# Softmax normalisation of seven groups and five weight casts moved to GpSimd, with a new order of the whole program

## The chip, the cores and the metric

The kernel runs on one core of a Trainium2 chip. The metric is the device time of one execution in microseconds. The core has five engines that work side by side, each through its own list of instructions in order: TensorE (PE in the profile; its weight loads are PEld), VectorE (DVE), ScalarE (ACT), GpSimd (POOL) and SyncE (SP), which here issues most DMAs. An instruction waits where something that it needs is not there yet, and everything behind it on its engine waits with it.

## The reference

Local attention with block summaries, and behind it a feed-forward network with a squared ReLU:

```python
k_sum = k.reshape(B, H, nb, block, D).max(axis=3)
v_sum = v.reshape(B, H, nb, block, D).mean(axis=3)
scores_l = scale * (q @ k^T), kept where |i - j| < 16
scores_s = scale * (q @ k_sum^T) + log(32)
a = softmax(concatenate([scores_l, scores_s]))
x = a @ concatenate([v, v_sum])      # 4 batches, 8 heads, 768 tokens, 64 wide
h = x @ w_in                         # 3072 tokens, 512 -> 2048
out = (max(h, 0) ** 2) @ w_out       # 2048 -> 512
```

Everything is float32; weights and activations are split into a high part and a low part, the rest, and each product is done as three.

## The kernel before

The tokens are cut into 48 groups of 64 (`g`), all heads of a group together. Per group the kernel does: scores on TensorE (`S`), the masked maximum on VectorE (`X` or `M`), exponentials with their sums on ScalarE (`E`), the reciprocal of the sums on VectorE (`R`), the normalisation of the probabilities (`N`), their transposition on TensorE (`T`) with a copy back by ScalarE (`A`), and the product with the values on TensorE (`V`). The result goes as high and low part (`XH` on ScalarE, `XL` on VectorE) into the buffers `xh` and `xl`. `KC` copies the 24 key maxima beside the next group's keys, on GpSimd; the scores of the next group wait for it. `LS` copies the 24 value sums beside a group's values; GpSimd does six of these copies.

Eight groups make a unit of 512 tokens. Units 0 and 1 go through the network plainly, in 16 steps (`FI` into the hidden layer, ReLU `RL`, square `SQ`, high part `GH`, low part `GL`, and `FO` out of it). The first two steps of unit 0 are halved, `a` for groups 0 to 3 and `b` for groups 4 to 7, so that work can begin before all eight groups are done. The last four units are done in two pairs by a folded scheme with seven products of half size instead of eight; its products (`SP`, `FP`) start when unit 1 is through, in the same PSUM banks, which the copies `PC` have to empty first.

A weight block is loaded as raw 64-bit words (`WL`) and turned into a high and a low part: `WM` rebiases the exponent on ScalarE, `WR` shifts the low word and `WJ` joins both on VectorE, `WH` makes the high part on ScalarE (line 1148), `WW` the low part on VectorE.

No loop sets the order. Every piece of work is a task with a due time, a cost and its predecessors; a planner (`Plan.order`) runs through time and lets each engine take the ready task with the smallest key. What it takes is written out, and each engine executes its list in this order. The due times come from constants (`T0`, `VISITS`, `SUMS`, `COMBS` and others), and a table `NUDGE` shifts single tasks.

The normalisation has three forms, chosen for each group by a letter of `NORMAL_BY`. On VectorE (`D`, line 911) it is one multiplication with the reciprocals spread over 118 columns each; on ScalarE (`A`) and on GpSimd (`P`) it is four instructions. No group has the letter `P` before the change. Its form is:

```python
def normal_by_pool():
    for p in range(NPAIR):
        x = pr.tile[:, p, :KEYS]
        nc.gpsimd.tensor_scalar(
            out=x, in0=x, scalar1=nm.tile[:, 2 * NPAIR + p : 2 * NPAIR + p + 1], scalar2=None, op0=ALU.mult
        )
```

Of the kernel before, what the change touches and what calls it, by code (L numbers as in the profile page):

```python
# [42 lines left out]
FIRST_LS = -147  # L43
# [7 lines left out]
NORMAL_BY = 'DDDDDDDDDDDDAADDDDDAADDADAAAADADDADAADADAAAAADAA'  # L51
NUDGE = {
# [15 lines left out]
SUMS_AT = (49.58, 98.461, 159.985)  # L68
HALVED = 2
TURN_LATE = 0.4  # L70
COMBS = (113.899, 126.88, 138.513, 154.582, 177.64, 218.83, 204.98, 217.58)
Q_LEAD = 2.06
XS_LEAD = 6
R_LEAD = 59
TR_LEAD = -6.51
VISITS = (50.338, 57.836, 69.578, 80.836, 104.683, 120.84, 136.81, 147.692, 155.7, 174.797, 185.163, 207.631, 229.485, 242.25, 269.184, 274.88, 306.59, 333.33, 368.58, 382.85, 404.251, 380.898, 406.82)
X_LEAD = 32.91
SPLIT_AT = -65.86
KEPT = (107.051, 3.085)
GH_LEAD = 10  # L80
# [117 lines left out]
class Plan:  # L198
# [14 lines left out]
        KC=(0.2, 0.2), LS=(0.5, 0.5), LD=(0.4, 0.4), N=(0.3, 1.4),  # L213
# [142 lines left out]
def attention_then_relu2_ffn(  # L356
# [95 lines left out]
    T0, SLOW, STEP = 23.88, 6.38, 6.62  # L452
    MIXED_STEP = (1.651, 1.487)
    X_BY = (19.133, 7.867)
    SUMS = (113.265, 126.664, 155.006, 159.6, 204.148, 201.393, 199.633, 202.628, 150.871, 186.465, 171.605, 168.63, 184.229, 220.694, 192.63, 206.893)
    PRODUCT_STEP = (1.392, 1.383)
    A0, A1, B0, B1 = 2.8, 4.14, 31.36, -0.93
    HALF_AT = (26.697, 30.498)
# [350 lines left out]
    def softmax(g, by_pe=False):  # L809
# [8 lines left out]
        one = g < ONE_EXP  # L818
        if g < EARLY + 2:

            t_c = add(
                f"C{g}", "POOL", 0.15, lambda: nc.gpsimd.memset(pr.tile[:, :, KEYS:], 0.0), due - 16,
                [] if early else t_S[g][:1], take=[] if early else [pr], use=[pr] * early, behind=t_QL[g],
            )
        for i, t_s in enumerate(t_S[g]):
# [38 lines left out]

# [236 lines left out]
    def convert(f, ns):  # L1101
# [16 lines left out]
        def temp():  # L1118
            return t.tile[:, : k * DM]
# [45 lines left out]
        t6 = add(f"WH{name}", "ACT", 0.08 + 0.43 * k, high, due - 6, [t4], take=[w], use=[t])  # L1165
# [11 lines left out]
    def ffn(u, f, o, done, half=None):  # L1177
# [34 lines left out]
        t4 = add(f"GH{name}", "ACT", act, lambda: nc.scalar.copy(out=cut(gh), in_=cut(r)), due + 5, [t3], take=[gh], use=[r])  # L1212
# [782 lines left out]
```

## Time and profile before

| | before |
|---|---|
| median of 3 runs | 574.42 us (572.8 to 574.7) |
| profiled execution | 573.33 us |
| its span, first to last instruction | 571.5 us |
| TensorE busy in the span | 558.2 us (98%) |
| VectorE busy | 466.0 us (82%) |
| ScalarE busy | 373.5 us (65%) |
| GpSimd busy | 46.7 us (8%) |
| mean granted TensorE clock | 0.999 of its full speed |

The busy share of an engine is an average over stages with different limits. What a change in a stage is worth is read from that stage: which engine is full there, and which wait ends last.

### The profile page before, as it was taken

How to read it: one execution, taken by the hardware profiler on the slowest of the kernel's cores; microseconds unless marked ns; L12 is line 12 of the kernel's file. 1: busy time of each engine (PE TensorE's matmuls, PEld its weight loads, DVE VectorE, ACT ScalarE, POOL GpSimd, SP SyncE). 2: the span in 40 equal slices, each digit the busy share in tenths (PEclk: the TensorE clock that was granted, in tenths of full speed). 3: DMA queues.
4: the chain of work that ended last, by engine and by line, in shares of the span. 5: the costliest groups of instructions: out<-in, count | busy, mean ns of one | idle time of the engine just before them, and what ended most of it. 6: DMA issues, size and time to landing. Idle time of an engine off the chain costs nothing.

```text
span 571.5 us, 11786 instructions
## 1 busy us (share of the span) xinstructions
PE 558.2 (98%) x3920; PEld 457.6 (80%) x3920; DVE 466.0 (82%) x1182; ACT 373.5 (65%) x968; POOL 46.7 (8%) x95
## 2 busy tenths in 40 slices
PE   7989999999999999999999999999999999999996
PEld 6668888878888888878788888888888888888885
DVE  4999999677899999989998997887583556868863
ACT  2899999577786978697766757465365542454442
POOL 4410031311001130000020000000000000000000
PEclk9999999999999999999999999999999999999999
DMA  8999999989999999999999887968975766767772
GB/s 295 377 397 358 324 288 295 291 234 379 385 293 326 299 370 358 343 350 335 285 278 298 257 266 212 280 194 262 273 212 162 187 197 189 195 193 233 189 233 96
DMA packets 86789, 157.01 MB, mean 275 GB/s; under 512 B 9064, under 2 KB 30506, under 8 KB 86730
## 3 DMA queue, kind: packets, MB, share of 16 engines
q1 hardware_dynamic: 85001, 151.70, 81.3%
q0 software_dynamic: 1728, 4.57, 5.1%
q8 instruction: 31, 0.51, 0.4%
q14 instruction: 29, 0.23, 0.1%
HBM read 112.00 MB, written 49.79 MB: 283 GB/s over the span
## 4 chain that ended last, share of the span: by engine, by line
PE 91%; DVE 4%; DMA 3%; issue 0%; ACT 0%; SPq 0%; DVEq 0%
PE o L1523 23%; PE o L1225 15%; PE o L1740 14%; PE h L1201 14%; PE sz L1740 7%; PE att L1523 4%; PE x L1011 4%; PE att L759 3%; PE sa L1740 3%; PE att L1740 2%; DMA q<-qW 1%; DMA kb<-kT 1%; DMA fv_lent<-vS 1%; DVE qvpa_lent L911 1%; PE o L759 1%; PE t L940 1%
## 5 line engine op out<-in xcount | busy, mean ns | idle before, releaser
L1505 ACT CAST gh<-g 128x512 fp32r<-128x512 f32 x112 | 69.4, 622 | 64.7 <-DVE gl L1510 31.7
L1523 PE MATMUL o<-gh,w 128*128 128x512 f32 x384 | 103.0, 390 | 0.0
L1510 DVE TENSOR_TENSOR gl<-g,gh 128x512 fp32r<-128x512 f32 x112 | 76.4, 687 | 27.2 <-ACT gh L1505 26.6
L1523 PEld LDWEIGHTS o<-gh,w 128*128 128x128 f32 x384 | 71.8, 188 | 15.0
L1201 PE MATMUL h<-xh,w 128*128 128x512 f32 x240 | 74.7, 392 | 0.0
L1777 ACT ACTIVATE g<-g 128x512 f32<-128x512 f32 x60 | 37.7, 631 | 46.9 <-DVE g L1773 46.8
L890 ACT ACTIVATE p<-p,small 128x118 f32<-128x118 f32 x160 | 61.7, 393 | 2.0 <-DVE small L833 2.0
L1225 PE MATMUL o<-w,gh 128*128 128x512 f32 x240 | 61.8, 393 | 0.0
L1523 PE MATMUL o<-gl,w 128*128 128x512 f32 x192 | 59.1, 389 | 0.0
L1201 PEld LDWEIGHTS h<-xh,w 128*128 128x128 f32 x240 | 44.5, 188 | 9.3
L1225 PEld LDWEIGHTS o<-w,gh 128*128 128x128 f32 x240 | 44.4, 188 | 9.3
L1201 PE MATMUL h<-xl,w 128*128 128x512 f32 x120 | 46.8, 390 | 0.0
L1523 PEld LDWEIGHTS o<-gl,w 128*128 128x128 f32 x192 | 36.0, 188 | 7.5
L1740 PE MATMUL o<-w,w 128*128 128x512 f32 x160 | 41.1, 393 | 0.3 <-DVE g L1765 0.3
L1740 PEld LDWEIGHTS o<-w,w 128*128 128x128 f32 x160 | 29.7, 188 | 6.8 <-DVE g L1765 0.7
L1740 PE MATMUL sz<-xh,w 128*128 128x512 f32 x128 | 34.2, 389 | 0.0
L1225 PE MATMUL o<-w,gl 128*128 128x512 f32 x120 | 33.6, 389 | 0.0
L833 DVE CUSTOM_DVE_ANT_0 p<-att,mask 128x118 f32<-128x118 f32 x152 | 32.7, 274 | 0.0
L1500 DVE TENSOR_TENSOR g<-g 128x512 f32<-128x512 f32 x48 | 32.4, 683 | 0.1
L1773 DVE CUSTOM_DVE_ANT_0 g<-sz,g 128x512 f32<-128x512 f32 x32 | 21.9, 684 | 12.3 <-ACT g L1760 6.9
L890 ACT ACTIVATION_READ_ACCUMULATOR p<-p,small 128x1 f32 x160 | 31.5, 197 | 0.0
L1740 PE MATMUL o<-xh,w 128*128 128x512 f32 x112 | 30.2, 391 | 0.8 <-DVE os L1262 0.8
(193 smaller groups left out, 1096.6 us busy)
## 6 DMA issues: line engine op xcount, KB each, us to landing
raw<-wW SPq DMA_DIRECT2D x32, 512.0 KB
w<-scr_t SPq DMA_DIRECT2D x64, 256.0 KB
w<-scr_s SPq DMA_DIRECT2D x64, 256.0 KB
w<-scr_a SPq DMA_DIRECT2D x48, 256.0 KB
w<-scr_i SPq DMA_DIRECT2D x44, 256.0 KB
turn<-a SPq DMA_DIRECT2D x17, 512.0 KB
scr_t<-ci SPq DMA_DIRECT2D x16, 512.0 KB
v<-vS SPq DMA_DIRECT2D x34, 192.0 KB
```

Source lines behind the costliest of these rows:

```text
L759: nc.tensor.matmul(score_at(g, part, j)[c * TQ : (c + 1) * TQ, :], lhsT=q_bufs[g].tile[rows, p, :] if term else unscale[rows, :], rhs=(mas ...
L833: nc.vector.tensor_tensor_reduce(out=pr.tile[:, j, :KEYS], in0=score_at(g, 0, j), in1=mask_of(g)[0], scale=-SCALE, scalar=-NEG, op0=ALU.ad ...
L890: nc.scalar.activation(x, score_tile(g, p % parts)[:, p] if by_pe else x, AF.Exp, bias=nm.tile[:, p : p + 1], scale=SCALE if by_pe else -1 ...
L1011: nc.tensor.matmul(x_of(i)[h % 2 * D : (h % 2 + 1) * D, h // 2, :], lhsT=v_bufs[g].tile[:KEYS, h * D : (h + 1) * D], rhs=av[:KEYS, 2 * c : ...
L1201: nc.tensor.matmul(cut(h), lhsT=lhs.tile[:, k // 2, k % 2 * P : (k % 2 + 1) * P], rhs=rhs[:, k, c0 : c0 + n], start=(i == 0), stop=(i == 3 ...
L1225: nc.tensor.matmul(o_of(o, t).rearrange("p (h c) -> p h c", h=2), lhsT=terms[i][0].tile[:, (t - t0) * P : (t - t0 + 1) * P], rhs=terms[i][ ...
L1500: lambda x=x, ins=ins, op=op: nc.vector.tensor_tensor(out=x.tile, in0=ins[0].tile, in1=ins[1].tile, op=op),
L1505: f"GH{s}_{n}", "ACT", 0.54, lambda x=x, gh=gh: nc.scalar.copy(out=gh.tile, in_=x.tile), due - GH_LEAD, ready,
L1510: lambda x=x, gh=gh, gl=gl: nc.vector.tensor_tensor(out=gl.tile, in0=x.tile, in1=gh.tile.bitcast(F32), op=ALU.subtract),
L1523: nc.tensor.matmul(o.tile[:, d], lhsT=chunk.tile[:, w * HALF + d * P : w * HALF + (d + 1) * P], rhs=y.tile, start=begins and w == 0 and y ...
L1740: nc.tensor.matmul(o.tile, lhsT=lhs(w, k), rhs=y[k], start=begins and i == 0, stop=i == 5, skip_group_check=not begins,)
L1777: f"G{name}_{s}", "ACT", 0.57, lambda: nc.scalar.activation(to.tile, to.tile, AF.Square), key + 0.7, [t], use=[to]
```

## The change

Groups 0 to 6 are normalised on GpSimd instead of VectorE. Five high parts of the first weight blocks (`WH0_1`, `WH1_0`, `WH0_2`, `WH1_1`, `WH1_2`) are made on GpSimd instead of ScalarE; the same table could move `GH` casts and another one a scaling, but no entry does. The planner knows for these GpSimd tasks how long they keep VectorE out. All constants that set due times are new, and so is the table of single shifts, which is shorter. The products and their number do not change.

```diff
-FIRST_LS = -147
+FIRST_LS = -153.244
...
-NORMAL_BY = 'DDDDDDDDDDDDAADDDDDAADDADAAAADADDADAADADAAAAADAA'
+NORMAL_BY = 'PPPPPPPDDDDDAADDDDDAADDADAAAADADDADAADADAAAAADAA'
 NUDGE = {
...
-    "SP.KL0_1": -3.5, "SP.KL3_1": 11.5, "SP.LV1": 2.2, "SP.LV3": 1.1, "SP.SL0_18": -11.1, "SP.SL0_2": 3.3, "SP.TR33_3": 26,
+    "DVE.GL0_13": 14, "DVE.M11b": 3.8, "DVE.R8": 104.4, "DVE.SCi1_0": 5.2, "DVE.WJ3": -28.2, "DVE.WR1_1": 3.2, "DVE.WR3": 84.7, "PE.SP0_1": 4,
...
 }
+SCALED_BY_POOL = ()
+HIGH_BY_POOL = '0_1', '1_0', '0_2', '1_1', '1_2'
...
-SUMS_AT = (49.58, 98.461, 159.985)
+SUMS_AT = (42.088, 91.605, 173.084)
...
-        KC=(0.2, 0.2), LS=(0.5, 0.5), LD=(0.4, 0.4), N=(0.3, 1.4),
+        KC=(0.2, 0.2), LS=(0.5, 0.5), LD=(0.4, 0.4), N=(0.3, 1.4), WH=(0.5, 1.0), GH=(0.5, 0.5), XC=(0.1, 0.1),
...
-    T0, SLOW, STEP = 23.88, 6.38, 6.62
+    T0, SLOW, STEP = 25.356, 6.244, 6.246
...
-    A0, A1, B0, B1 = 2.8, 4.14, 31.36, -0.93
+    A0, A1, B0, B1 = -38.506, -18.174, -33.444, -11.133
...
+        by_pool = name in HIGH_BY_POOL
+
         def high():
-            nc.scalar.copy(out=part(0, w.tile), in_=by_n(temp()))
+            if not by_pool:
+                nc.scalar.copy(out=part(0, w.tile), in_=by_n(temp()))
+                return
+            for i in range(k):
+                at = slice(2 * i, 2 * i + 2)
+                nc.gpsimd.tensor_copy(out=part(0, w.tile)[:, at], in_=by_n(temp())[:, at])
...
-        t6 = add(f"WH{name}", "ACT", 0.08 + 0.43 * k, high, due - 6, [t4], take=[w], use=[t])
+        t6 = add(f"WH{name}", "POOL" if by_pool else "ACT", 0.6 * k if by_pool else 0.08 + 0.43 * k, high, due - 6, [t4], take=[w], use=[t])
```

GpSimd, in the start phase, before: it copies key maxima (`kb`, the tasks `KC`) and value sums (`fv` into `qvpa`, the tasks `LS`; the digit behind `qvpa` is the group).

```order
L772 COPY kb_73<-kb_73 128x4x24 x2
L714 COPY qvpa0_lent_145<-fv1_lent_270 24x512
L714 COPY qvpa1_lent_171<-fv1_lent_270 24x512
L772 COPY kb_73<-kb_73 128x4x24
L714 COPY qvpa2_lent_196<-fv1_lent_270 24x512
L714 COPY qvpa5_lent_351<-fv1_lent_270 24x512
L714 COPY qvpa3_lent_267<-fv1_lent_270 24x512
```

The same place after, from the normalisation of group 2 to the first two weight casts (the rows of line 927 are the normalisations, four instructions each):

```order
L927 TENSOR_SCALAR qvpa2_lent_221<-qvpa2_lent_221,small3_86 128x118 x4
L711 COPY qvpa1_lent_194<-fv1_lent_274 24x512
L927 TENSOR_SCALAR qvpa3_lent_265<-qvpa3_lent_265,small1_72 128x118 x4
L711 COPY qvpa3_lent_265<-fv1_lent_274 24x512
L711 COPY qvpa2_lent_221<-fv1_lent_274 24x512
L711 COPY qvpa0_lent_146<-fv1_lent_274 24x512
L711 COPY qvpa5_lent_364<-fv1_lent_274 24x512
L769 COPY kb_73<-kb_73 128x4x24
L927 TENSOR_SCALAR qvpa4_lent_314<-qvpa4_lent_314,small2_85 128x118 x4
L711 COPY qvpa7_lent_293<-fv1_lent_274 24x512
L769 COPY kb_73<-kb_73 128x4x24
L1159 CAST w0_1_569<-t0_1_509 128x2x256
```

Three normalisations now stand between the copies, and the copy of key maxima that the scores of group 5 need stands behind two of them and five copies.

ScalarE, before, around group 5's exponentials (`qvpa5`): the transposed copies (line 947) of groups 3 and 4 come behind them.

```order
L1068 CAST xh_74<-att1_69 128x4x64
L890 ACTIVATE qvpa5_lent_351,small3_86<-o0_66,small3_86 128x118
L1068 CAST xh_74<-att0_68 128x4x64
L890 ACTIVATE qvpa5_lent_351,small3_86<-o0_66,small3_86 128x118 x3
L1134 ACTIVATE t0_1_551<-raw0_1_391 128x512
L947 COPY qvpa3_lent_267<-t3_543 128x4x4x32
L890 ACTIVATE qvpa6_lent_229,small1_72<-o1_67,small1_72 128x118 x4
L947 COPY qvpa4_lent_312<-t4_555 128x4x4x32
L1148 CAST w1_0_610<-t1_0_502 128x2x256
```

After, at the same place (the copies are line 951):

```order
L951 COPY qvpa3_lent_265<-t3_480 128x4x4x32
L1138 ACTIVATE t1_0_494<-raw1_0_351 128x512
L1138 ACTIVATE t0_1_509<-raw0_1_398 128x512
L1072 CAST xh_74<-att1_69 128x4x64
L1072 CAST xh_74<-att0_68 128x4x64
L951 COPY qvpa4_lent_314<-t4_549 128x4x4x32
L894 ACTIVATE qvpa5_lent_364,small3_86<-o0_66,small3_86 128x118 x4
```

Both transposed copies now stand ahead of group 5's exponentials, and the weight cast is gone from the list.

TensorE, where unit 1 ends and the folded products begin, before: the last piece of step 15 (line 1225, bank `o0`), the first folded product (line 1740) in that bank, and then scores of a visit (line 759).

```order
L1225 MATMUL o0_66<-w15_1526,gh1_15_3148 128x512 x2
L1225 MATMUL o0_66<-w15_1526,gl1_15_3157 128x512
L1740 MATMUL o0_66<-xh_74,w5_954 128x512 x4
L1740 MATMUL o0_66<-xl_75,w5_954 128x512 x2
L759 MATMUL att0_68<-kb_73,q34_3048 64x118
```

After, at the same place (lines 1238, 756, 1015 and 1753; of the sixteen rows of scores the first and the last):

```order
L1238 MATMUL o0_66<-w15_1590,gh1_15_3147 128x512 x2
L1238 MATMUL o0_66<-w15_1590,gl1_15_3151 128x512
L756 MATMUL att0_68<-kb_73,q34_3004 64x118
L756 MATMUL att1_69<-kw35_3256,q35_3214 64x118
L1015 MATMUL x31_3292<-a15_2989,v0_80 64x64 x8
L1015 MATMUL x31_3292<-a15_2989,v1_81 64x64 x8
L1753 MATMUL o0_66<-xh_74,w5_1029 128x512 x4
```

A whole visit, scores of two groups and values of two others, has moved between the last piece of step 15 and the first folded product.

## Rows read from the trace of the kernel before

**Rows 1.** The page, part 1: busy time, share of the span, instructions.

```profile
PE 558.2 (98%) x3920; PEld 457.6 (80%) x3920; DVE 466.0 (82%) x1182; ACT 373.5 (65%) x968; POOL 46.7 (8%) x95
```

**Rows 2.** Busy time by stretch: length, then PE, PEld, DVE, ACT, POOL, clock, DMA share, GB/s.

```profile
20.00:30.00 10.00, 9.29 (x212) 7.60 (x208) 9.64 (x27) 9.53 (x41) 5.72 (x11) 1.00 1.01 374
30.00:40.00 10.00, 7.44 (x100) 5.92 (x100) 9.75 (x41) 10.00 (x33) 0.85 (x3) 1.00 1.03 394
40.00:100.00 60.00, 60.00 (x442) 49.72 (x443) 59.55 (x139) 58.65 (x139) 8.17 (x8) 1.00 0.99 321
```

**Rows 3.** What TensorE waited for in the whole span: total, times, longest.

```profile
PE o L1740 <- DVE os L1262: 0.8, 1, 0.8
```

**Rows 4.** Timeline of TensorE at the change to folded products: start, length, work.

```profile
245.94 1.20 PE L1740 MATMUL o<-xh,w 128*128 128x512 f32 x4 [0.78 <-DVE os L1262]
...
247.53 0.63 PE L759 MATMUL att<-kb,q 64*64 64x118 f32 x16
...
249.57 1.19 PE L1740 MATMUL o<-xh,w 128*128 128x512 f32 x4
```

**Rows 5.** Timeline of TensorE in the start phase.

```profile
26.24 0.66 PE L940 MATMUL t<-ident,qvpa_lent 128*128 128x128 f32 x4
...
42.48 0.40 PE L1201 MATMUL h_1b<-xh,w 128*128 128x256 f32 x2
...
45.36 1.09 PE L1225 MATMUL o<-w,gh_1a 128*128 128x512 f32 x4
...
46.74 0.61 PE L1201 MATMUL h<-xh,w 128*128 128x512 f32 x2
```

**Rows 6.** Timeline of ScalarE in the start phase.

```profile
19.35 0.36 ACT L890 ACTIVATE qvpa_lent<-o,small 128x118 f32<-128x118 f32 x1 [0.78 <-PE vps L639]
...
28.10 0.36 ACT L890 ACTIVATE qvpa_lent<-o,small 128x118 f32<-128x118 f32 x1 [0.27 <-DVE small L902]
...
29.45 0.60 ACT L947 COPY qvpa_lent<-t 128x512 f32<-128x512 f32 x1
29.92 0.65 ACT L1148 CAST w<-t 128x512 fp32r<-128x512 f32 x1
30.44 0.40 ACT L1068 CAST xh<-att 128x256 fp32r<-128x256 f32 x1
30.70 0.40 ACT L890 ACTIVATE qvpa_lent<-o,small 128x118 f32<-128x118 f32 x1
...
38.54 1.23 ACT L1134 ACTIVATE t<-raw 128x1024 f32<-128x1024 f32 x1
39.58 0.69 ACT L1148 CAST w<-t 128x512 fp32r<-128x512 f32 x1
...
41.63 0.53 ACT L1211 ACTIVATE rl_1a<-rl_1a 128x256 f32<-128x256 f32 x1
...
42.62 0.50 ACT L890 ACTIVATE p<-p,small 128x118 f32<-128x118 f32 x1
```

**Rows 7.** Timeline of VectorE in the start phase: a reciprocal, two normalisations.

```profile
19.36 0.18 DVE L905 RECIPROCAL small<-small 128x4 f32<-128x4 f32 x1
...
20.19 0.63 DVE L911 TENSOR_TENSOR qvpa_lent<-qvpa_lent,small 128x472 f32<-128x472 f32 x1
...
22.82 1.06 DVE L911 TENSOR_TENSOR qvpa_lent<-qvpa_lent,small 128x472 f32<-128x472 f32 x1
```

**Rows 8.** Timeline of GpSimd in the start phase: the copies that it makes there.

```profile
21.80 0.26 POOL L772 COPY kb<-kb 128x96 f32<-128x96 f32 x1
22.01 2.33 POOL L714 COPY qvpa_lent<-fv_lent 24x512 f32<-24x512 f32 x3
...
26.14 0.60 POOL L714 COPY qvpa_lent<-fv_lent 24x512 f32<-24x512 f32 x1
```

**Rows 9.** GpSimd by line and shape, whole span: count, busy us, mean ns, idle before.

```profile
L711 POOL TENSOR_SCALAR v<-v 24x512 f32<-24x512 f32 x6 | 9.4, 1572 | 28.1 <-DMA v<-scr_v 28.0
```

**Rows 10.** VectorE by line and shape from 8 to 120 us, the same columns.

```profile
L1143 DVE SCALAR_TENSOR_TENSOR t<-t,raw 128x1024 uint32<-128x1024 uint32 x13 | 15.8, 1219 | 0.0
```

More of the change, by code (lines that the diff above doesn't have):

```diff
@@ L67 @@
 PRODUCTS = 7
-SUMS_AT = (49.58, 98.461, 159.985)
+SUMS_AT = (42.088, 91.605, 173.084)
 HALVED = 2
 TURN_LATE = 0.4
-COMBS = (113.899, 126.88, 138.513, 154.582, 177.64, 218.83, 204.98, 217.58)
-Q_LEAD = 2.06
-XS_LEAD = 6
+COMBS = (115.229, 144.009, 117.536, 142.436, 172.103, 194.681, 219.406, 233.892)
+Q_LEAD = 41.536
+XS_LEAD = 27.332
 R_LEAD = 59
[L75 to L80, printed above, removed]
+TR_LEAD = 55.996
+VISITS = (46.093, 54.007, 61.05, 79.182, 86.042, 121.834, 129.822, 140.351, 158.348, 167.717, 189.929, 217.253, 252.25, 259.124, 281.547, 286.692, 303.002, 362.999, 384.958, 416.22, 365.382, 380.898, 406.82)
+X_LEAD = 20.632
+SPLIT_AT = -80.318
+KEPT = (111.743, 4.775)
+GH_LEAD = 40.705
 REBIAS = 2.0**-112
@@ L232, in order @@
             x = NUDGE.get(f"{t.engine}.{t.name}", 0.0)
-            t.key += x
-            if t.engine == "SP":
-                t.begin += x
+            t.key = round(t.key + x, 4)
+            t.begin = round(t.begin + x * (t.engine == "SP"), 4)
         then = {t: [] for t in self.tasks}
@@ L257, in order @@
             t.holds = self.HOLDS.get(kind) if t.engine == "POOL" else None
-            t.slack = self.SLACK.get(kind, 0.0) if t.key > -80 else 0.0
+            t.slack = 0.0 if t.name.startswith("KM0") else self.SLACK.get(kind, 0.0)
             t.size *= self.HEAVY.get(kind, 1.0)
@@ L449, in lend @@
         return [Part(b, i * DM, (i + 1) * DM, x) for i, x in enumerate(shapes or (None,) * 4)]
-    T0, SLOW, STEP = 23.88, 6.38, 6.62
[L453 to L456, printed above, removed]
-    A0, A1, B0, B1 = 2.8, 4.14, 31.36, -0.93
-    HALF_AT = (26.697, 30.498)
+    T0, SLOW, STEP = 25.356, 6.244, 6.246
+    MIXED_STEP = (1.538, 0.558)
+    X_BY = (28.615, 23.966)
+    SUMS = (90.104, 113.239, 171.614, 148.929, 181.242, 217.206, 196.604, 232.288, 122.574, 200.61, 167.904, 174.248, 211.347, 246.994, 214.967, 206.827)
+    PRODUCT_STEP = (1.98, 2.346)
+    A0, A1, B0, B1 = -38.506, -18.174, -33.444, -11.133
+    HALF_AT = (23.688, 30.554)
     MX = 0.95
@@ L818, in softmax @@
         one = g < ONE_EXP
+        scaled = by_pe and g in SCALED_BY_POOL
         if g < EARLY + 2:
@@ L853, in most, with scale @@
                 )
-                if by_pe and not one:
+                if by_pe and not one and not scaled:
                     nc.vector.tensor_scalar_mul(m, m, SCALE)
+            def scale(js=js):
+                m = nm.tile[:, :NPAIR][:, js]
+                nc.gpsimd.tensor_scalar(out=m, in0=m, scalar1=SCALE, scalar2=None, op0=ALU.mult)
             if not by_pe:
@@ L860, in softmax @@
                 t_x.append(add(
-                    f"X{name}", "DVE", 0.07 + 0.48 / parts + 0.2 * (by_pe and not one), most, due - 13, [t_m[-1]],
+                    f"X{name}", "DVE", 0.07 + 0.48 / parts + 0.2 * (by_pe and not one and not scaled), most, due - 13, [t_m[-1]],
                     take=[] if i else [nm], use=[x] + [nm] * bool(i),
                 ))
+                if scaled:
+                    t_x[-1] = add(f"XC{name}", "POOL", 0.25, scale, due - 12.95, [t_x[-1]], use=[nm])
             def less(i=i, js=js, nj=nj):
@@ L1211, in ffn @@
         t3 = add(f"SQ{name}", "ACT", act - 0.02, lambda: nc.scalar.activation(cut(r), cut(r), AF.Square), due + 4, [t2], use=[r])
-        t4 = add(f"GH{name}", "ACT", act, lambda: nc.scalar.copy(out=cut(gh), in_=cut(r)), due + 5, [t3], take=[gh], use=[r])
+        by_pool = f"g{name}" in HIGH_BY_POOL
+        copy = nc.gpsimd.tensor_copy if by_pool else nc.scalar.copy
+        t4 = add(f"GH{name}", "POOL" if by_pool else "ACT", act + 0.07 * by_pool, lambda: copy(out=cut(gh), in_=cut(r)), due + 5, [t3], take=[gh], use=[r])
         t5 = add(
```

3 lines of the change are left out of this document (2 added, 1 removed), and 5 rows, old and new, of the table NUDGE.

## The prediction

> **What bounds the kernel now.** I read the page's busy times first [rows 1]: TensorE is busy 558.2 us of a span of 571.5 us, so with the same instructions on it no change gains more than the 13.3 us in which it is not, and part of that is the start, where data must land, and the tail, where results must leave. Then the busy time by stretch [rows 2]: from 40 to 100 us TensorE has no gap at all; between 20 and 40 us it lacks 0.71 and 2.56 us, and there ScalarE is busy 9.53 and 10.00 us and VectorE 9.64 and 9.75 us of each 10. The start phase is therefore bounded by ScalarE and VectorE together, with ScalarE the fuller one, and the rest by TensorE. The list of TensorE's waits [rows 3] has one of size far behind the start phase: 0.8 us for the copy that empties unit 1's sums.
>
> The profiled execution took 573.33 us, its span and 1.83 us around it; the median of the three timed runs is 574.42 us, 1.09 us above it. I work out a difference against the profiled one and put it on the median. About 0.3%, 1.72 us, is what a measurement of this kernel can tell from no change.
>
> **Part 1: the change of units.** Before, TensorE goes from the last piece of FFN step 15 straight to a folded product into the same bank, and waits 0.78 us for the copy `PC` [rows 4]. In the changed order a whole visit (scores of groups 34 and 35, values of 30 and 31) stands between. Such a visit lasts 2.04 us in the row, from 247.53 to 249.57 [rows 4], longer than the wait. So this wait is covered: -0.78 us. If the copy is late by more than 1.3 us in the new VectorE order, the cover is gone and the term is 0.
>
> **Part 2: ScalarE's work in the start phase.** Everything that TensorE does before it may begin the second halves of steps 0 and 1 (42.48 us [rows 5]) hangs on `XH7`, the last of eight copies on ScalarE. I count what the new order has between the first exponential of group 3 (19.35 us [rows 6]) and `XH7`. Removed: four weight casts. One takes 0.52 us from its start to the next instruction's (29.92 to 30.44 [rows 6]), so 2.08 us. Added, because the new order has them earlier: one rebias of a 1024-wide weight, 1.04 us (38.54 to 39.58 [rows 6]); one square, one exponential and one cast of step 1, together 0.99 us (41.63 to 42.62 [rows 6]); one more exponential, 0.34 us (four took 28.10 to 29.45 [rows 6]). Together 2.37 us: `XH7` stands 0.29 us later in ScalarE's work, not earlier. But TensorE has by then also done the output product of step 1, 1.38 us (45.36 to 46.74 [rows 5]). TensorE's work is the same in both kernels, so that is a credit: -1.38 us. The idle 0.47 us that ScalarE had in this stretch [rows 2] is no part of the new sum either: -0.47 us. With no new wait on ScalarE the start would be 1.56 us shorter.
>
> **Part 3: the new wait, GpSimd's queue.** The changed order puts the transposed copy of group 4 (`A4`) ahead of group 5's exponentials. It waits for transposes, and these for the normalisation `N4`, now on GpSimd. Behind `A4` stand all later items of ScalarE, so its lateness goes to `XH7` in full.
>
> When would ScalarE be there? Before, from 19.35 to 30.70 us, it did in 11.35 us, less 0.47 idle, all that the new order has ahead of `A4`, and besides eight exponentials (2.70 us), `A4` (0.47, 29.45 to 29.92), a cast (0.52) and `XH3` (0.26, 30.44 to 30.70) [rows 6]. That leaves 6.93 us: it arrives at 26.28 us.
>
> When is `N4` done? The chain starts at the end of group 2's reciprocal, 19.54 us [rows 7]: three normalisations, five copies of value sums and one copy of key maxima, one behind the other on GpSimd. The key copy takes 0.26 us and a value copy 0.60 us alone, or 0.78 us (2.33 us for three) beside VectorE [rows 8]. A normalisation is four multiplications of 118 elements, and no row shows one. From below it is the 96-element copy, 0.26 us a piece. From above it is GpSimd's own multiplication, 1.57 us for 512 elements [rows 9]: the two copies give a slope of 0.82 ns an element and 0.18 us fixed, and (1.57 - 0.18) / 512 x 118 + 0.18 is 0.50 us. I take 0.32 us, nearer the copy, whose size and full set of partitions are the nearer ones.
>
> By that the chain is 3 x 1.28 + 5 x 0.65 + 0.26 = 7.35 us, `N4` ends at 26.89, the transposes take 0.66 us [rows 5], and `A4` waits from 26.28 to 27.55: +1.27 us. From below the chain is 6.38 us and the wait 0.30; from above 10.16 us and 4.08.
>
> The Trainium skill (GPSIMD Engine Reference, Engine selection) calls one-input elementwise work on GpSimd roughly line rate. The trace has both: the 512-element copy in 0.60 us agrees, the multiplication in 1.57 us does not. By that rule the wait would be near its lower bound and the time near the first rival's.
>
> **Part 4: what is costed at nothing.** The five casts on GpSimd: `WH0_1` stands right behind `N4`, two copies and group 5's queue, near 29 us, where ScalarE did it at 35.33; even at 1.57 us each they are early. VectorE loses seven normalisations, 4.4 us at 0.63 [rows 7], and is not the fuller engine, so I count nothing; what it may lose instead is a rival. The dues of all later stages are new, but from 40 us on TensorE is full in the rows [rows 2] and the other engines run ahead of it; I found no wait there but the one of part 1 that the new order touches with a price above 0.4 us.
>
> **Sum.** +0.29 - 1.38 - 0.47 + 1.27 = -0.29 us for the start, -0.78 us for the change of units: -1.07 us. 574.42 - 1.07 is 573.35; I say 573.4 us.
>
> **The rivals.**
> Rival 1, faster: GpSimd's pieces run at the copy's speed, the wait is 0.30 us, the start gains 1.26 and all gains 2.04 us: 572.4 us. If the shorter softmax chains also close the rest of TensorE's gaps between 20 and 40 us (3.27 us [rows 2]), it is 3.27 + 0.78 = 4.05 us: 570.4 us. For it: ScalarE and VectorE are both full there and both lose work. Against: GpSimd is one more engine in the chain of each group.
>
> Rival 2, slower: GpSimd's queue becomes the bound. At 0.50 us a piece the wait is 4.08 us, the start loses 2.52, and the whole 1.74 us: 576.2 us; 576.9 us if the wait of part 1 does not go either. It decides from a piece of 0.50 us with part 1's gain, and of 0.43 us without it. For it: the only multiplication in the trace is that slow [rows 9]. Against: those are on 24 partitions and 512 elements.
>
> Rival 3, slower or the same: VectorE and GpSimd block each other. A normalisation on VectorE that met GpSimd's copies took 1.06 us where the one before it took 0.63 [rows 7, 8], so 0.43 was lost; two were hit like this. VectorE has some 19 instructions with two inputs or in a doubled mode between group 2's reciprocal and the last `XL`. From there five normalisations go, 3.2 us, and the two old collisions, 0.86; a wide join comes in, 1.22 us [rows 10], and what else is moved is about even: 2.8 us less. At half a piece, 0.16 us, each they lose 3.0 us; the last `XL` is then 0.2 us late, covered by the credit of part 2, and the forecast stands. At 0.43 us each they lose 8.2 us, it is 5.4 us late, and the time is 5.4 - 1.38 - 0.78 = 3.2 us more: 577.6 us. The loss passes 1.72 us from 0.35 us each. The Trainium skill (SBUF — State Buffer, Who interferes with whom) states such a rule: a VectorE instruction with two SBUF inputs and a GpSimd instruction that reads SBUF exclude each other, and the later one waits for the whole of the other. The 1.06 us row agrees with it; that the pieces are short is what speaks against the full price.
>
> **How the numbers follow.** The forecast has 0.48, rival 1 has 0.35, rival 2 has 0.10 and rival 3's slow end 0.07. The predicted time is the forecast's, 573.4 us; its own range, for waits from 0.6 to 2.5 us, is 572.7 to 574.6. The range that holds 8 in 10 reaches down to 570.4, the end of rival 1, and up to 576.4, just over the lower price of the slow cases. Faster by over 0.3%, which is under 572.7, is rival 1: 0.35. Slower by over 0.3%, over 576.1, is rivals 2 and 3: 0.17. Within 0.3%: 0.48.
>
> **What would show it.** In the changed profile, GpSimd's multiplication of 118 elements should be near 0.32 us; ScalarE should be idle a little over 1 us before the transposed copy that follows two rebiases; TensorE should begin the second half of step 0 near 43.6 us; and no wait for the copy of the sums should be left at the change of units. The prediction is wrong if a piece is near 0.26 or near 0.50 us, if `A4` is not where ScalarE waits, or if TensorE has new waits behind 45 us, which I priced at nothing.

## The result: slower, and the profile after

| | before, in the same comparison | after |
|---|---|---|
| median | 574.08 us (572.8 to 574.7, 4 runs) | 579.23 us (577.29 to 579.54, 4 runs) |
| profiled execution, its span | 573.33 us, 571.5 us | 579.06 us, 576.9 us |
| mean granted TensorE clock of the runs | 0.999 (profiled) | 0.990 to 0.993 |

The ratio after to before is 1.0084, with a 95% interval from 1.0065 to 1.0102: slower by some 5 us, above the range of the prediction. The first part of the page of after answers to [rows 1]:

```profile
PE 563.6 (98%) x3920; PEld 461.4 (80%) x3920; DVE 465.0 (81%) x1175; ACT 373.5 (65%) x963; POOL 67.6 (12%) x128
```

TensorE does the same 3920 instructions in 5.4 us more. GpSimd has 20.9 us more work. VectorE, which gave seven normalisations away (6.0 us for eight before, 0.6 for the one left), is busy only 1.0 us less: its other instructions take 4.4 us longer. The stretches of [rows 2], after:

```profile
20.00:30.00 10.00, 7.92 (x108) 5.40 (x104) 6.06 (x19) 6.99 (x26) 10.00 (x19) 0.87 0.96 312
30.00:40.00 10.00, 9.11 (x151) 7.20 (x148) 7.99 (x22) 6.72 (x30) 8.22 (x15) 0.79 1.02 392
40.00:100.00 60.00, 58.36 (x478) 47.34 (x478) 57.20 (x155) 56.21 (x140) 12.69 (x20) 1.00 0.90 296
```

From 20 to 30 us GpSimd, the fifth number, is busy 10.00 of 10 us, and VectorE and ScalarE, which were full there, only 6.06 and 6.99. The bound has gone to GpSimd. The column behind GpSimd is the granted clock, 0.87 and 0.79 where it was 1.00. Finer stretches show where it fell:

```profile
8.00:10.00 2.00, 0.45 (x12) 0.40 (x12) 1.32 (x2) 0.00 (x0) 0.27 (x4) 1.00 1.04 402
10.00:12.00 2.00, 2.00 (x14) 1.90 (x10) 1.64 (x4) 1.01 (x5) 0.00 (x0) 0.59 1.07 397
12.00:14.00 2.00, 2.00 (x20) 1.78 (x23) 0.90 (x2) 1.08 (x2) 0.00 (x0) 0.56 1.04 386
...
26.00:28.00 2.00, 0.90 (x3) 0.32 (x3) 0.77 (x4) 1.52 (x7) 2.00 (x4) 0.85 0.99 322
28.00:34.00 6.00, 5.86 (x84) 4.80 (x84) 4.33 (x7) 2.65 (x7) 6.00 (x12) 0.50 0.97 340
```

Twice TensorE stood (busy 0.45 of 2 us from 8 to 10, 0.90 of 2 from 26 to 28), and behind it the clock went to the lower of its two levels, 1.2 GHz in place of 2.4. A busy TensorE at 0.50, as from 28 to 34 us, does half the work: eight score products take 0.39 us from start to start at 30.89 us and 0.20 at 36.22. The Trainium skill (TensorE: Matmul & The Clock Gate, HAM oscillation — how this bites in real kernels) tells of the same: waits between short bursts let the clock fall, and the next burst starts slow. These rows agree.

GpSimd by line and shape, whole span (count, busy us, mean ns, idle before):

```profile
L927 POOL TENSOR_SCALAR qvpa_lent<-qvpa_lent,small 128x118 f32<-128x118 f32 x28 | 18.5, 675 | 2.0 <-DVE small L909 1.8 <-ACT qvpa_lent L894 0.2
...
L1159 POOL CAST w<-t 128x512 fp32r<-128x512 f32 x5 | 3.4, 692 | 5.6 <-ACT gh_1b L1225 4.6 <-DVE t L1147 1.0
```

A normalising piece takes 0.675 us in the mean; I had it at 0.32, with 0.50 as the upper bound. GpSimd's timeline (L927 the normalisations, L711 value sums, L769 key maxima) shows the queue:

```profile
16.45 2.29 POOL L927 TENSOR_SCALAR qvpa_lent<-qvpa_lent,small 128x118 f32<-128x118 f32 x4 [0.67 <-DVE small L909]
...
19.23 2.27 POOL L927 TENSOR_SCALAR qvpa_lent<-qvpa_lent,small 128x118 f32<-128x118 f32 x4 [0.21 <-ACT qvpa_lent L894]
...
21.68 2.28 POOL L927 TENSOR_SCALAR qvpa_lent<-qvpa_lent,small 128x118 f32<-128x118 f32 x4
23.90 0.60 POOL L711 COPY qvpa_lent<-fv_lent 24x512 f32<-24x512 f32 x1
24.48 2.50 POOL L927 TENSOR_SCALAR qvpa_lent<-qvpa_lent,small 128x118 f32<-128x118 f32 x4
26.93 2.27 POOL L711 COPY qvpa_lent<-fv_lent 24x512 f32<-24x512 f32 x4
29.15 0.77 POOL L769 COPY kb<-kb 128x96 f32<-128x96 f32 x1
29.90 2.76 POOL L927 TENSOR_SCALAR qvpa_lent<-qvpa_lent,small 128x118 f32<-128x118 f32 x4
```

From 21.68 us no row has an idle time: each instruction waits only for the one ahead of it. `N4` ends at 32.66 us. ScalarE stands 2.70 us for what hangs on it, `A4`, and TensorE begins the second half of step 0 (`h_0b`) at 50.23 us, where I had expected 43.6, and stands 0.75 us in it:

```profile
33.23 0.59 ACT L951 COPY qvpa_lent<-t 128x512 f32<-128x512 f32 x1 [2.70 <-PE t L944]
```

```profile
50.23 0.50 PE L1212 MATMUL h_0b<-xh,w 128*128 128x256 f32 x2 [0.36 <-ACT xh L1072]
51.48 0.39 PE L1212 MATMUL h_0b<-xl,w 128*128 128x256 f32 x1 [0.75 <-DVE xl L1075]
```

The same work of the start (both halves of the first product of steps 0 and 1, and the first halves of their second) is done at 54.31 us after and at 46.74 before [rows 5]: 7.57 us later. From there to the last product's end it is 518.26 us after (to 572.57) and 520.48 before (to 567.22): 2.22 us less. The rows that begin the rest and end it, after, and the row that ends it before:

```profile
54.31 0.64 PE L756 MATMUL att<-kb,q 64*64 64x118 f32 x16
...
572.18 0.39 PE L1536 MATMUL att<-gl,w 128*128 128x512 f32 x1
```

```profile
566.83 0.39 PE L1523 MATMUL att<-gl,w 128*128 128x512 f32 x1
```

The wait at the change of units [rows 4] is among what went: from 52 us on the list of TensorE's waits is empty. TensorE's timeline from the last piece of step 15, through the visit, to the first folded product in bank `o`:

```profile
251.73 0.39 PE L1238 MATMUL o<-w,gl 128*128 128x512 f32 x1
252.05 0.64 PE L756 MATMUL att<-kb,q 64*64 64x118 f32 x16
...
253.02 1.15 PE L1015 MATMUL x<-a,v 118*64 118x64 f32 x32
254.10 1.19 PE L1753 MATMUL o<-xh,w 128*128 128x512 f32 x4
```

### The profile page after: what moved, and what is told of

Its sections match the earlier page's. It is cut to its first block, busy times and chain, and to the rows that moved or that the text cites. A ratio compares the mean times of both kernels' runs of the same rounds, so it can differ in the third digit from the quotient of the medians.

```text
span 576.9 us, 11813 instructions
## 1 busy us (share of the span) xinstructions
PE 563.6 (98%) x3920; PEld 461.4 (80%) x3920; DVE 465.0 (81%) x1175; ACT 373.5 (65%) x963; POOL 67.6 (12%) x128
## 4 chain that ended last, share of the span: by engine, by line
PE 92%; POOL 2%; DVE 2%; DMA 1%; issue 1%; ACT 0%; SPq 0%; POOLq 0%; ACTq 0%
PE o L1536 23%; PE o L1238 15%; PE h L1212 14%; PE o L1753 14%; PE sz L1753 8%; PE x L1015 4%; PE att L1536 4%; PE att L756 3%; PE sa L1753 3%; PE att L1753 2%; POOL qvpa_lent L927 2%; DMA kb<-kT 1%; PE o L756 1%; PE t L944 1%; PE warm L552 1%
```

## Experiments

Theory 1: GpSimd's price for a normalisation holds the start back (my second rival's mechanism, with a larger price). Theory 2: the new first loads, which put the keys `KL0_3` first and let TensorE stand from 7 to 9.5 us, and the clock that falls behind this gap. Theory 3: the weight casts on GpSimd, or GpSimd and VectorE in each other's way. Each ratio is to the kernel before in the same comparison.

| run | median us (lowest to highest, runs) | ratio, 95% interval | mean clock of the runs |
|---|---|---|---|
| n_dve | 575.92 (572.3 to 580.6, 10) | 1.0039 [1.0002, 1.0077] | 0.988 to 1.000 |
| before_p | 581.52 (578.31 to 583.11, 4) | 1.0120 [1.0062, 1.0179] | 0.992 to 0.996 |
| kl_n_dve | 573.22 (571.95 to 576.54, 10) | 0.9990 [0.9965, 1.0014] | 0.997 to 1.000 |
| one_tt | 578.00 (573.75 to 580.96, 10) | 1.0076 [1.0044, 1.0108] | 0.988 to 1.000 |
| kl | 579.34 (577.28 to 583.28, 4) | 1.0123 [1.0080, 1.0166] | 0.988 to 0.992 |
| n_dve_warm | 573.30 (572.04 to 573.88, 10) | 1.0004 [0.9993, 1.0015] | 0.998 to 1.000 |
| kl_one_tt | 573.79 (572.85 to 575.37, 10) | 1.0021 [1.0006, 1.0036] | 0.995 to 1.000 |
| replan_d_kl | 592.90 (592.75 to 593.46, 4) | 1.0353 [1.0336, 1.0370] | 0.981 to 0.984 |
| after_warm | 577.72 (576.43 to 578.09, 4) | 1.0081 [1.0060, 1.0102] | 0.993 to 0.997 |
| warm_wh_act | 575.06 (574.01 to 580.23, 12) | 1.0039 [1.0016, 1.0061] | 0.990 to 1.000 |
| n_early | 574.66 (574.10 to 576.72, 12) | 1.0033 [1.0018, 1.0048] | 0.992 to 1.000 |
| n3_early | 575.09 (572.87 to 576.24, 12) | 1.0019 [0.9998, 1.0039] | 0.993 to 1.000 |
| before_gap | 575.05 (573.49 to 576.70, 10) | 1.0012 [0.9991, 1.0032] | 0.997 to 1.000 |
| n4_early | 572.97 (571.52 to 576.43, 12) | 0.9998 [0.9982, 1.0014] | 0.998 to 1.000 |

**n_dve**: the normalisations back on VectorE, in the order of the change.

```diff
-t_n = add(f"N{g}", "POOL", 1.4, normal_by_pool, due - 10, [t_r], use=[pr, nm])
+t_n = add(f"N{g}", "POOL", 1.4, normal, due - 10, [t_r], use=[pr, nm])
```

> The changed kernel's order kept as it is; only the seven early normalisations (groups 0 to 6) are issued to VectorE again, as one broadcast product of 128x472 each (0.56 to 0.64 us there), in place of four GpSimd pieces of 0.59 us. Theory 1 (GpSimd is too slow: a normalisation takes it 2.3 to 3.2 us, its queue holds the start phase back): from the changed kernel's 579.2 us some 4 to 6 us come back, so 573 to 575 us; GpSimd is busy under 9 of 10 us in 20 to 30 us, the granted clock does not fall to 0.50 between 26 and 36 us, and the first second-half product of unit 0 begins near 46 us, not 50.2. Theory 2 (the new order of the first loads and the clock that falls at 10 to 14 us cost the time): at most 1 us comes back, 578 to 579 us, and the second half still begins after 49 us. Theory 3 (the weight casts on GpSimd and the two engines' contention): no change beyond 1 us.

In the profiled run (572.3 us) `h_0b` begins at 44.28 us, the mean clock is 1.000 and this run takes no more time than before. But the ten runs reach up to 580.6 us, and most of the long ones have low mean clocks; none of the long ones was profiled. By the middle ratios (1.0084 to 1.0039) the pieces have a good half of the loss, though the two intervals overlap; something else comes and goes from run to run.

**before_p**: the kernel before, in its order, with the GpSimd form for groups 0 to 6.

```diff
-t_n = add(f"N{g}", "DVE", 0.56, normal, due - 10, [t_r], use=[pr, nm])
+t_n = add(f"N{g}", "DVE", 0.56, normal_by_pool if g < 7 else normal, due - 10, [t_r], use=[pr, nm])
```

> The kernel before with its order kept; only the normalisations of groups 0 to 6 are issued to GpSimd as four pieces each, so 28 pieces; weight casts, dues and first loads stay as before. Theory 1: 28 pieces of 0.59 us are 16.5 us of work on a queue that also turns halves of the keys and makes copies; TensorE waits on GpSimd before the turns of the probabilities, the clock falls to 0.50 in some stretch before 40 us, and the time is 576.5 to 580 us. Theory 2: the first loads are those of before, so the time stays within 1 us of 574.1. My predicted price (0.32 us a piece) would give 573.5 to 575 us.

The pieces alone, with none of the new loads, casts or dues, cost as much as the whole change, if not more (the intervals overlap). Its windows:

```profile
20.00:26.00 6.00, 4.77 (x116) 3.72 (x108) 4.82 (x14) 5.53 (x22) 6.00 (x12) 1.00 1.03 368
26.00:30.00 4.00, 2.02 (x39) 1.59 (x39) 1.36 (x6) 1.97 (x8) 4.00 (x8) 1.00 0.99 389
```

GpSimd is full and the others stand, here at the full clock, which falls only later (0.58 from 40 to 44 us). So the queue costs time by itself, before any fall.

**kl_n_dve** and **kl**: without the shift of one load (the rest is planned again by the same rules), the first with, the second without the normalisations on VectorE.

```diff
-    "POOL.LS0": -8.9, "POOL.LS1": -33.6, "POOL.ident": -91.8, "SP.KL0_3": -12.9, "SP.SL0_0": 9.3,
+    "POOL.LS0": -8.9, "POOL.LS1": -33.6, "POOL.ident": -91.8, "SP.SL0_0": 9.3,
```

> The changed kernel's plan without the shift of one load (keys KL0_3) ahead of the others, planned again, and the seven normalisations issued to VectorE. Theories 1 and 2 both undone: if the start's new load order is worth its own 1 to 2 us, this lies 1 to 2 us below the run with the normalisations on VectorE alone, at 571 to 573.5 us, the first exponentials begin near 9.5 us, not 10.9, and the clock holds at 10 to 14 us. If the load order costs nothing, the two agree within 0.5 us.

> The changed kernel planned again without the shift that puts the load of keys KL0_3 first; the seven normalisations stay on GpSimd as four pieces each. Theory 1 (GpSimd's slow pieces are the cost): 577 to 579.5 us, GpSimd busy 5.5 of 6 us or more in 20 to 26 us, the second half of a step begins after 48 us. Theory 2 (the new first loads and the clock's fall are the cost): 573 to 575 us, the clock holds at 10 to 14 us. Both: about half of each, 576 to 577 us.

With the pieces on GpSimd the load order is worth nothing: 1.0123 without the shift, 1.0084 with it. Windows of kl: no fall at 10 to 14 us, but the one behind GpSimd's full queue is there.

```profile
10.00:14.00 4.00, 2.63 (x52) 1.53 (x52) 2.91 (x6) 1.69 (x5) 0.70 (x4) 1.00 1.05 394
20.00:26.00 6.00, 4.76 (x62) 3.01 (x61) 3.34 (x12) 4.34 (x19) 6.00 (x13) 0.93 1.02 350
26.00:30.00 4.00, 3.37 (x63) 3.23 (x64) 2.65 (x5) 2.47 (x5) 4.00 (x8) 0.50 0.90 292
```

With the normalisations on VectorE (kl_n_dve) no mean clock is under 0.997, and the time is that of before. The step from kl to kl_n_dve, 0.0133 with intervals far apart, is the clearest measure of the pieces.

**n_dve_warm** and **after_warm**: twelve more filler products ahead of the first scores, in the gap from 7 to 9.5 us, with the normalisations on VectorE and on GpSimd.

```diff
-nc.tensor.matmul(x.tile, lhsT=ident, rhs=ident, start=True, stop=True)
+for _ in range(2 if i < WARM else 1):
+    nc.tensor.matmul(x.tile, lhsT=ident, rhs=ident, start=True, stop=True)
```

> The changed kernel with the seven normalisations on VectorE (575.9 us, with runs from 572.3 at a mean clock of 1.000 to 580.6 at 0.988), and each of the twelve filler products ahead of the first scores issued twice, so that TensorE has no gap between 7 and 9.5 us; nothing else is changed. If the gap in TensorE's work there is what lets the granted clock fall in some executions, and the fall costs the time, the mean clock is 0.997 or more in all runs, their spread falls to that of before (about 3 us), and the median to 572.5 to 574 us. If the clock falls for another reason (the sparse stretch at 20 to 30 us), the spread stays and the median is 575 to 577 us.

> The changed kernel with its normalisations on GpSimd as they are, and each of the twelve filler products ahead of the first scores issued twice; nothing else. With the normalisations on VectorE this took 2.6 us off. Theory 1 alone (GpSimd's queue, and the clock that falls at 24 to 36 us behind it): 578 to 580 us, as without the filler. If the fall at 10 to 14 us adds its cost to GpSimd's: 576 to 577.5 us.

TensorE from 7 to 10 us, first in n_dve, then in n_dve_warm:

```profile
7.00:10.00 3.00, 1.43 (x20) 1.05 (x20) 2.28 (x4) 0.00 (x0) 1.12 (x8) 1.00 1.03 401
```

```profile
7.00:10.00 3.00, 2.77 (x33) 2.27 (x32) 2.28 (x4) 0.00 (x0) 1.12 (x8) 1.00 1.03 402
```

With VectorE normalising, the ratio falls from 1.0039 to 1.0004 where the gap is filled, and the spread of the runs from 8.3 to 1.8 us; kl_n_dve, the other run without the gap, has 0.9990. So the gap seems to cost some 0.35% there, but this is not clear of the noise: the intervals overlap, and the two runs stand in different comparisons, in which the kernel before itself spreads over 5.4 and 3.5 us. Nor does the filler keep the clock up everywhere: warm_wh_act, n_early and n3_early have it too, and mean clocks down to 0.990.

With the pieces on GpSimd the times show nothing (1.0081 against 1.0084). The traces do: the clock is at 1.00 from 10 to 14 us, GpSimd's queue begins 1.46 us earlier (group 2 at 20.22 us, not 21.68), and the start's work is done at 52.82 us, 1.49 us earlier; the profiled span is 0.8 us shorter. From after_warm:

```profile
20.22 2.27 POOL L928 TENSOR_SCALAR qvpa_lent<-qvpa_lent,small 128x118 f32<-128x118 f32 x4
```

```profile
52.82 0.63 PE L757 MATMUL att<-kb,q 64*64 64x118 f32 x16
```

**one_tt** and **kl_one_tt**: one product of two inputs on GpSimd in place of four pieces.

```diff
-for p in range(NPAIR):
-    x = pr.tile[:, p, :KEYS]
-    nc.gpsimd.tensor_scalar(
-        out=x, in0=x, scalar1=nm.tile[:, 2 * NPAIR + p : 2 * NPAIR + p + 1], scalar2=None, op0=ALU.mult
-    )
+x = pr.tile[:, :, :KEYS]
+nc.gpsimd.tensor_tensor(
+    out=x, in0=x, in1=nm.tile[:, 2 * NPAIR : 3 * NPAIR].unsqueeze(2).broadcast_to([P, NPAIR, KEYS]), op=ALU.mult
+)
```

> The changed kernel, with each early normalisation on GpSimd as one product of two inputs over 128x472 (the factor broadcast along the keys) in place of four pieces of 128x118. No row so far shows this form on GpSimd. If a piece's 0.59 us is mostly a fixed cost of an instruction, one normalisation falls from 2.3 us to 1.0 to 1.6 us and theory 1 gives 575 to 577.5 us. If it is by elements (472 at the 3.1 ns an element of the 512-wide row is 1.45 us, and a second input may add as much again: 2.9 us), it gives 576 to 581 us. Theory 2: no change, 578.5 to 580 us, whatever the instruction takes.

> The changed kernel without the shift of load KL0_3, and with each early normalisation on GpSimd as one product over 128x472 (0.98 us in the run before this) in place of four pieces (2.3 to 3.2 us). If the four pieces' price is all that is wrong with the change's idea, GpSimd is no longer full in 20 to 30 us and the time is 572 to 574 us, not above the kernel before; if GpSimd is still too slow for the place (0.98 against 0.56 us on VectorE, and handed over between engines), 574.5 to 577 us.

One normalisation now takes 0.98 us in place of 2.3 to 3.2:

```profile
L926 POOL TENSOR_TENSOR qvpa_lent<-qvpa_lent,small 128x472 f32<-128x472 f32 x7 | 6.9, 980 | 6.2 <-DVE small L909 6.2
```

With the gap in the loads left in, this gains nothing that can be told (1.0076 against 1.0084); in the profiled run, one of the long ones (580.67 us), the clock fell behind the gap:

```profile
7.00:9.00 2.00, 0.42 (x4) 0.20 (x4) 1.89 (x3) 0.00 (x0) 1.16 (x8) 0.96 1.05 404
9.00:14.00 5.00, 4.65 (x28) 4.17 (x28) 2.75 (x6) 1.97 (x6) 0.00 (x0) 0.50 1.05 400
```

With the gap out, the time is 1.0021 of before; the intervals with and without it lie apart, so here the price of the new first loads and their gap is clear, as far as two different comparisons allow. The pieces without the gap have 1.0123 in the same comparison. So most of the loss by the pieces, some 0.0102 of the 0.0123, was their form, not the move to GpSimd. Either one, the pieces or the gap, is enough to lose by; only with both gone is the time near that of before.

**forms**: GpSimd's price by form and size; groups 0 to 2 by one instruction with one factor a row (it leaves out the factors of three of the four pairs), groups 3 to 6 by four small products of two inputs.

```diff
+if g < 3:
+    x = pr.tile[:, :, :KEYS]
+    nc.gpsimd.tensor_scalar(out=x, in0=x, scalar1=nm.tile[:, 2 * NPAIR : 2 * NPAIR + 1], scalar2=None, op0=ALU.mult)
+    return
+for p in range(NPAIR):
+    x = pr.tile[:, p, :KEYS]
+    f = nm.tile[:, 2 * NPAIR + p : 2 * NPAIR + p + 1].broadcast_to([P, KEYS])
+    nc.gpsimd.tensor_tensor(out=x, in0=x, in1=f, op=ALU.mult)
```

> A look at GpSimd's price by form, not a version: without the shift of load KL0_3, groups 0 to 2 are scaled by one GpSimd instruction with one factor a row over 128x472 (so the four pairs of those groups get the first pair's factor, which is not what the kernel computes), and groups 3 to 6 by four products of two inputs over 128x118 each. If the 0.58 us of a piece is a fixed cost of every GpSimd instruction, the small products take 0.55 to 0.6 us and the one wide one near 1 us. If the form with a factor for each row is slow by element, the wide one takes 1.5 to 2.3 us and the small products 0.25 to 0.45 us. The time itself, with one look, is told apart only beyond 2 us: 574 to 580 us by either.

```profile
L932 POOL TENSOR_TENSOR qvpa_lent<-qvpa_lent,small 128x118 f32<-128x118 f32 x16 | 6.5, 432 | 2.7 <-ACT xh L1075 1.3 <-ACT t L1141 1.0 <-DVE small L909 0.4
L927 POOL TENSOR_SCALAR qvpa_lent<-qvpa_lent,small 128x472 f32<-128x472 f32 x3 | 4.4, 1468 | 2.8 <-DVE small L909 2.8
```

and one group of four small products in GpSimd's timeline:

```profile
20.82 1.40 POOL L932 TENSOR_TENSOR qvpa_lent<-qvpa_lent,small 128x118 f32<-128x118 f32 x4
```

The form with a factor a row takes 1.47 us for 472 elements and 0.57 for 118, which fits a fixed cost of some 0.27 us and 2.5 ns an element, an estimate from these two; the product takes 0.98 and, at best, 0.35. The one run took 574.55 us.

**warm_wh_act**: n_dve_warm with the five casts on ScalarE again (the GpSimd branch of `high` left out).

> The run with normalisations on VectorE and the filler doubled (573.3 us), with the five early high parts of weights cast on ScalarE again, at the places that they have in the change's order. Theory 3 (the casts on GpSimd cost something): faster by 0.5 us or more, under 572.8 us. If moving the casts is worth something: ScalarE, busy 9.6 of 10 us at 40 to 50 us, gets some 3 us more, and the time is 574 to 576 us. If they lie beside other work either way: 573 to 573.8 us.

It is slower, 1.0039 against 1.0004: in this order the casts on GpSimd are a useful part of the change, worth some 2 us (0.0035 of 573; the two intervals leave 0.6 to 3.4). Its profile has the clock at 0.74 from 30 to 36 us, but its four runs at a mean clock of 1.000, 574.01 to 575.29 us, are slower too. Theory 3 falls for the casts; that GpSimd and VectorE stand in each other's way was not tested by a run of its own.

**n_early, n3_early, n4_early**: n_dve_warm with normalisations moved ahead in VectorE's queue: all seven, that of group 3, that of group 4.

```diff
+todo.insert([t.name for t in todo].index("R4") + 1, n)   # n: the task N4, taken out of its place
```

> The run with normalisations on VectorE and the filler doubled (573.3 us), with each of the seven normalisations put right behind its own reciprocal in VectorE's queue, where the change's order has it one to three instructions later (the fourth stood behind a join of weights that waits 0.69 us for ScalarE, and ScalarE stood 1.33 us for it). Every other engine's order is kept. If that place is what is left of the change's loss at the start: the copy of the turned probabilities begins 1 to 1.6 us earlier, the second half of unit 0 begins near 43.2 us, not 44.5, and the time is 571.8 to 572.6 us, below the kernel before. If something else ends last there: 573 to 573.8 us.

> The run with normalisations on VectorE and the filler doubled (573.3 us), with the fourth group's normalisation alone put right behind its reciprocal in VectorE's queue, ahead of the join of weights that waits 0.69 us for ScalarE; the others stay where the change has them. If its place keeps the start late: ScalarE's idle of 1.33 us ahead of the copy of that group's turned probabilities is gone, and the time is 571.8 to 572.8 us, 0.1 to 0.3% below the kernel before. If the clock falls again at 26 to 32 us, or another wait takes its place: 573 to 575 us.

> As n3_early, but with the normalisation of group 4 (the fifth), which is the one that stood behind the waiting join of weights, put right behind its reciprocal. If its place keeps the start late: it runs near 24.9 us, not 26.5, ScalarE's idle of 1.33 us ahead of the copy of that group's turned probabilities is gone, the second half of unit 0 begins 0.8 to 1.4 us earlier, near 43.4 us, and the time is 571.9 to 572.7 us. If the maxima and the scores of group 5 end last there anyway (ScalarE waits 0.79 us for them too): 573 to 573.8 us, as with the filler alone.

n_early put `N0` ahead of the next group's maxima, for which the exponentials wait, and was slower; that this is the reason is my reading (in its profile the clock is also at 0.50 from 28 to 30 us). n3_early moved the wrong one: the instruction that I had seen behind the join was `N4`. n4_early moved that, and ScalarE's idle ahead of `A4` fell from 1.33 to 0.77 us; the next wait then grew from 0.79 to 1.35:

```profile
27.99 0.58 ACT L952 COPY qvpa_lent<-t 128x512 f32<-128x512 f32 x1 [0.77 <-PE t L945]
29.92 0.36 ACT L895 ACTIVATE qvpa_lent<-o,small 128x118 f32<-128x118 f32 x1 [1.35 <-DVE small L854]
```

So the maxima of group 5 end last there, and the time is that of before. n3_early's 1.0019 cannot be told from it. No version beat the kernel before by more than its interval.

**before_gap**: the kernel before with eight filler products left out.

> The kernel before with eight of the twelve filler products ahead of the first scores left out (they compute nothing that is used), so that TensorE stands still from about 5 to 8 us; the order is kept. If a gap there lets the granted clock fall and the fall costs the time, as the runs of the changed kernel's order say: mean clocks of 0.997 or less in most runs, and 574.5 to 577 us. If the clock's fall needs more than the gap, or costs nothing in this order: within 0.7 us of the kernel before, 572.8 to 574 us.

Inconclusive: seven of the ten runs have a mean clock of 0.997 and the median is 575.05 us, as the first case had it; but TensorE was busy only 0.54 of 3 us from 4 to 7 us and the granted clock of the profiled run stayed at 1.00, and the ratio's interval holds 1. Whether a gap there costs time stays open.

**replan_d_kl**: the table gives groups 0 to 6 to VectorE, without the shift of the load, all planned again.

```diff
-NORMAL_BY = 'PPPPPPPDDDDDAADDDDDAADDADAAAADADDADAADADAAAAADAA'
+NORMAL_BY = 'DDDDDDDDDDDDAADDDDDAADDADAAAADADDADAADADAAAAADAA'
```

> The changed kernel with the normalisations of groups 0 to 6 given to VectorE in the table itself, so that the plan's times count them there, and without the shift of load KL0_3; the five weight casts stay on GpSimd and the later due times are those of the change. If the order planned for the right engine matters, it is faster than the run with the order of the change and VectorE normalising (573.2 us): 570.5 to 572.5 us; if not, 572.5 to 574 us. Theory 3 (weight casts on GpSimd cost something): over 574.5 us.

It was expected by none of the cases; that it is over 574.5 us, as theory 3 has it, comes from another engine. Its list of TensorE's waits begins with a weight cast on ScalarE:

```profile
PE h L1212 <- ACT w L1155: 14.7, 1, 14.7
```

The due times were searched with the other table, and the order that the planner makes of them here puts that cast late. It tells nothing of GpSimd; that the numbers of a plan hold only together is my reading and was not tested further.

## Why the prediction was wrong

**Part 3, the term +1.27, failed by its price.** The mechanism was there: GpSimd's queue, `N4`, `A4`, ScalarE behind it. But I took a piece at 0.32 us, from the 96-element copy, and the upper bound of 0.50 us was no bound: it gave the multiplication [rows 9] the copies' fixed cost of 0.18 us. Four pieces in a row took 2.27 us undisturbed (19.23 us in the timeline), 0.57 each. With that my own sum gives 3 x 2.27 + 5 x 0.65 + 0.26 = 10.32 us, `N4` at 29.86, a wait of 4.24 us in place of 1.27, and 573.35 + 2.97 = 576.3 us: rival 2's place and sign, from a price above the point where I said that it decides. The row nearer in operation, not the one nearer in size, was the one to take.

**What that sum still lacks**, 2.9 us to 579.2. By the profiled spans it is 3.5 us (5.4 measured, 1.90 by the sum), and the rows place it, from one profile each. I took the end of group 2's reciprocal, 19.54 us, over from before; in the new order it is 21.25, and `N2` begins at 21.68, 2.14 us late:

```profile
21.07 0.18 DVE L909 RECIPROCAL small<-small 128x4 f32<-128x4 f32 x1
```

In after_warm `N2` begins at 20.22, so 1.46 of this go with the gap in the first loads and the clock's fall behind it; the other 0.68 come with a queue that `N0` and `N1` had held since 16.45 us, which I followed from group 2 on only. From `N2`'s start to `N4`'s end it then took 10.98 us in place of 10.32, with `N3`, `N4` and the key copy longer than alone, beside VectorE at work. `A4` began 0.57 us behind `N4`, where I had 0.66, so in all it was 2.71 us later than in the sum (ScalarE itself came to it at 30.53 us, not 26.28, so only 2.70 us show as its wait). From there the start took 21.08 us (33.23 to 54.31) where the prediction has 18.90: 2.18 us more, of which 0.75 is TensorE's wait for the last `XL`. Against this, the later stages gave 2.22 us, not 0.78. The half clock from 28 to 34 us lies beside GpSimd's full queue, and no row shows what it cost there.

**The Trainium skill's line** (GPSIMD Engine Reference, Engine selection), by which one-input work there runs at roughly line rate, would have had the time near rival 1. The multiplication by a factor a row says otherwise: 1.47 us for 472 elements, where the two-input product takes 0.98.

**Part 1 held**: the change of units has no wait; later stages together took 2.22 us less. **Part 2** counted ScalarE's work well but none of its waits. In n_dve_warm ScalarE is ready for `A4` at 26.63 us, where I had 26.28; but it stands there for 1.33 us and behind it for 0.79, with the normalisations on VectorE:

```profile
27.96 0.58 ACT L952 COPY qvpa_lent<-t 128x512 f32<-128x512 f32 x1 [1.33 <-PE t L945]
29.34 0.36 ACT L895 ACTIVATE qvpa_lent<-o,small 128x118 f32<-128x118 f32 x1 [0.79 <-DVE small L854]
```

So the start that was to be 1.56 us shorter without a new wait is 1.07 us longer there. **Part 4** named the casts' cover rightly (TensorE waits for none of them), but missed the first loads, with which TensorE stands from 7 to 9.5 us. **Rival 3** is seen on both engines: the last two normalisations took GpSimd 3.21 and 3.19 us in place of 2.27 while VectorE was at work, and VectorE's seven small multiplications of 128x4 (line 853, before line 855) took 354 ns in the mean in place of 181. The late last `XL` is there too, 0.75 us of it; on VectorE it stands behind a wide join:

```profile
49.90 1.19 DVE L1147 SCALAR_TENSOR_TENSOR t<-t,raw 128x1024 uint32<-128x1024 uint32 x1
51.01 0.42 DVE L1075 TENSOR_TENSOR xl<-att,xh 128x256 fp32r<-128x256 f32 x1
```

With pieces and gap both gone the changed order takes the time of before (1.0004): what the later stages give, the start's new order takes. In n_dve_warm's profile the start's work is done at 47.81 us, 1.07 us later than before, and the rest takes 519.73 us, 0.75 less.

## What to carry to other kernels

Before work moves to an engine that is nearly idle, price it by a row of the same operation and operand kinds on that engine, not by one of the same size, and give an upper bound its own fixed cost. Add up the new engine's queue from the first item that goes into it, with everything that stands in line there, and do not take the times at which work arrives over from the old order. Count an engine's waits as well as its work. Where TensorE is made to wait, the price can be more than the wait: look at the granted clock right behind it, in more than one run.

## What the runs showed of the hardware

GpSimd's product of two inputs is cheaper than its multiplication of one input by a factor a row: 0.98 us against 1.47 for 128x472, and four of 128x118 took 1.40 us at best against 2.27. For the second form 24 partitions cost as much as 128: 1.57 us for 512 elements [rows 9] and 1.47 for 472, 3.1 ns an element in both, all told. GpSimd and VectorE take longer beside each other: four pieces took 2.27 us beside a lightly used VectorE and 3.21 beside a busy one.

The granted clock falls in some executions of one kernel and not in others. The ten runs of n_dve go from 572.3 us at a mean of 1.000 to 580.6 at 0.988; the order is not strict (579.44 at 0.997), so the clock is not all of the spread. The kernel before does it too, though seldom: its five longest runs took 577.16 to 578.46 us at 0.992 to 0.996. And not every stand of TensorE is followed by a fall: in before_p it was busy 2.02 of 4 us from 26 to 30, and the clock stayed at 1.00 up to 40 us; in n_dve's profile 1.43 of 3 from 7 to 10, and it stayed at 1.00 as well.
